# Half-array matmul pairs for kv, nd and the last rows of the two token matmuls, in a kernel of linear attention and an MLP mixer

## The chip, the cores and the metric

The kernel runs on one core of a Trainium2 chip. The metric is device time in microseconds (us), the median of several executions. All runs reported here are set against runs of the kernel before from the same rounds on the same chip. The profile's span is some 2 us shorter than the device time; spans are compared with spans only. The engines have these names in the profile: PE is TensorE (the 128 x 128 array that does the matmuls), ACT is ScalarE, DVE is VectorE, POOL is GpSimd, and SP issues transfers. PSUM is the memory that matmuls write to and ACT and DVE read from; a tile there is called a buffer below. A *mode* of the array is the way it is cut: whole, in two halves of 64 columns, or in two halves of 64 rows.

## The reference, cut to what matters

```python
# q, k, v: (8, 8, 576, 64)
q_p, k_p = phi(q), phi(k)                        # where(x > 0, x, exp(x) - 1) + 1
kv  = einsum('bhsd,bhse->bhde', k_p, v)          # "kv"
z   = sum(k_p, axis=2)
num = einsum('bhsd,bhde->bhse', q_p, kv)         # "nd": num and den in one matmul
den = einsum('bhsd,bhd->bhs', q_p, z)[..., None] + 1e-06
x   = (num / den) as (8, 576, 512)
h   = relu(x^T @ w_tok1) @ w_tok2                # "mm1", "mm2": over the 576 tokens
u   = x + h^T
out = u + relu(u @ w_ch1) @ w_ch2                # "mm3", "mm4": the wide ones
```

A batch has 576 = 4 x 128 + 64 tokens. The last 64 ("tail", row group R = 4) fill half of the 128 partitions; two batches share a tile for them in mm3 and mm4, so the natural period of the kernel is a **pair of batches**.

## The kernel before

Steady work is a list of wide pieces (mm3 and mm4, matmuls of 512 columns). Small pieces for the next batch are put between them by number: after wide step i come the pieces with number i, sorted in a stable way. This one order is the order of issue for every engine.

```python
def kv(n, g, first=False):                   # g: half of the heads; ps: 128 x 4*65 of PSUM
    for i in range(2):
        j = 2 * g + i                        # a pair of heads in one full matmul
        for r in range(R1):
            nc.tensor.matmul(out=ps[:, i], lhsT=kp[:, r, 2*j:2*j+2, :],
                             rhs=(vst[b] if r == R else vs[:, r])[:, 2*j:2*j+2, :],
                             start=(r == 0), stop=(r == R))
    for i in range(2):                       # only the diagonal blocks are wanted
        nc.scalar.copy(out=kvbd[b][half[i], 2*g:2*g+2, i*D1:(i+1)*D1],
                       in_=ps[half[i], :, i*D1:(i+1)*D1])

def nd_mm(n, g, rs):                         # six pieces a batch: 2 halves x ([0,1], [2,3], [4])
    for i, r in enumerate(rs):
        for a in range(2):
            nc.tensor.matmul(out=ps[:, i, ...], lhsT=qT[b][:, 2*g+a, r, :],
                             rhs=kvbd[b][:, 2*g+a, :], start=True, stop=True)
# ... nd_end (DVE): den + eps, reciprocal, multiply into x
# ... mm1: 2 x 5 matmuls of 512 columns, then two relus on ACT; mm2: DVE adds x, giving u
# ... mm2 of the tail: 2 matmuls a batch with zero-padded weights w2t, one DVE add into ut
# ... utr: 16 transposes of u, copied to uT by ACT and DVE

def run(bigs, fill):
    for i, big in enumerate(bigs):
        big()
        for s, fn in fill:
            if s == i: fn()

def fill_of(n, at, ks, qs):
    fill += [(at[nm], fn) for nm, fn in steps(n + 1)]                     # next batch
    fill += [(s, lambda g=g: prep_k(n + 2, g)) for g, s in enumerate(ks)] # ks = [10, 12]
    fill += [(s, lambda g=g: prep_q(n + 2, g)) for g, s in enumerate(qs)]
    return sorted(fill, key=lambda e: e[0])
# prep_k: ACT exp, DVE add/min/max, ACT casts of v

AT = {"kv0": 0, "kv1": 1, "qt0": 2, "qt1": 3, "nd00": 4, "nd01": 5, "nd10": 6, "nd11": 7,
      "nd20": 8, "nd21": 9, "mm1": 11, "mm2a": 14, "mm2b": 15, "mm2t": 16, "ut": 17, "utt": 19}
```

## Time and profile before

| | before |
|---|---|
| device time, median of 3 | 293.16 us (292.76 to 293.96); 293.38 with a fourth run below |
| span of the profile | 290.8 us |
| TensorE busy | 274.4 us (94%) |
| DVE, ACT busy | 58%, 57% |
| period of a pair of batches | 64.31 us |

The period is the distance between the first kv matmul of one batch and that of the batch two later, read from TensorE's timeline (132.37 and 196.68 us).

### The profile page before, as it was taken

Reading aid. Unit: us, or ns where it says so; the run is one execution under the profiler, and the core shown is the slowest. Engines: PE = TensorE matmul, PEld = TensorE weight load, DVE = VectorE, ACT = ScalarE, POOL = GpSimd, SP = SyncE. Lnnn points to the kernel's source line nnn. Section 1 sums busy time; section 2 is a strip of 40 time slices with the busy share of each in tenths; the row PEclk is TensorE's granted clock in tenths of the full one; section 3 lists DMA queues with packets and bytes.
Section 4 is the critical chain, followed back from the end, with each engine's and each line's share of the span. In section 5 each row is a group of like instructions: output and inputs, shape, how many; then the busy total and the mean of one; then the engine's idle time right before and its main releaser. Section 6 shows DMA issues by size and latency. Waiting matters only on the chain.

```text
span 290.8 us, 5019 instructions
## 1 busy us (share of the span) xinstructions
PE 274.4 (94%) x2002; PEld 156.5 (54%) x2002; DVE 168.2 (58%) x329; ACT 164.7 (57%) x254; POOL 29.3 (10%) x52
## 2 busy tenths in 40 slices
PE   8888987978999899999999999999999999999993
PEld 8776444543754465456565465456565464544641
DVE  5885377585657948692859517791769334530021
ACT  3663875139983676756696086658694185026400
POOL 3080030012000210010000210010001200000000
PEclk9999999999999999999999999999999999999999
DMA  6999999999996970785066710011001210011031
GB/s 204 280 139 202 300 241 211 293 283 359 278 291 207 287 206 2 212 239 184 0 169 204 261 39 0 36 69 42 2 0 38 108 36 2 36 72 38 1 108 72
DMA packets 46231, 41.84 MB, mean 144 GB/s; under 512 B 14656, under 2 KB 43200, under 8 KB 46208
## 3 DMA queue, kind: packets, MB, share of 16 engines
q1 hardware_dynamic: 39712, 30.68, 37.0%
q0 software_dynamic: 6496, 10.85, 15.8%
q8 instruction: 15, 0.25, 0.4%
q14 instruction: 8, 0.07, 0.1%
HBM read 35.85 MB, written 9.44 MB: 156 GB/s over the span
## 4 chain that ended last, share of the span: by engine, by line
PE 72%; DMA 11%; SPq 5%; ACT 4%; DVE 3%; issue 2%; POOL 1%; ACTq 0%
PE h_ps L359 28%; PE c_ps L336 22%; DMA q_raw<-in_q_dram 7%; PE a_ps L231 5%; PE h_ps L242 4%; DMA wc<-in_moe_w_ch_dram 3%; SPq L106 3%; PE nd_ps L196 3%; PE c_ps L347 3%; SPq L104 2%; PE tp L173 2%; PE tp L259 2%; PE kv_ps L163 2%; ACT e L116 2%; DMA k_raw<-in_k_dram 1%
## 5 line engine op out<-in xcount | busy, mean ns | idle before, releaser
L336 PE MATMUL c_ps<-uT,wc 128*128 128x512 bf16 x384 | 92.8, 379 | 2.4 <-ACT cr L340 1.5
L359 PE MATMUL h_ps<-wc,cr 128*128 128x512 bf16 x384 | 90.4, 379 | 0.0
L340 ACT ACTIVATE cr<-c_ps 128x512 bf16<-128x512 f32 x96 | 56.5, 599 | 47.4 <-PE c_ps L336 47.1
L359 PEld LDWEIGHTS <-cr 128*128 128x128 bf16 x384 | 36.5, 98 | 39.5
L336 PEld LDWEIGHTS <-wc 128*128 128x128 bf16 x384 | 35.4, 97 | 35.6 <-issue 3.3
L369 DVE TENSOR_TENSOR o_sb<-h_ps,u 128x512 f32<-128x512 f32 x32 | 21.8, 685 | 20.2 <-PE h_ps L359 20.1
L373 POOL DMA_DIRECT2D out_dram<-o_sb x24 | 14.4, 601 | 164.1 <-DVE o_sb L369 142.3
L209 DVE TENSOR_TENSOR x<-nd_ps,den 128x512 bf16<-128x512 f32 (+1 forms) x48 | 28.9, 603 | 1.7
L130 DVE TENSOR_SCALAR e<-e 128x1280 bf16<-128x1280 bf16 (+1 forms) x34 | 16.1, 474 | 22.0 <-ACT e L116 22.0
L206 DVE TENSOR_SCALAR den<-nd_ps 128x8 f32<-128x8 f32 (+1 forms) x48 | 7.8, 162 | 34.9 <-PE nd_ps L196 34.4
L116 ACT ACTIVATE e<-k_raw 128x1280 bf16<-128x1280 f32 x16 | 20.3, 1270 | 3.3 <-DMA k_raw<-in_k_dram 3.2
L116 ACT ACTIVATE e<-q_raw 128x1280 bf16<-128x1280 f32 (+1 forms) x18 | 20.3, 1150 | 2.8 <-DMA q_raw<-in_q_dram 2.7
L263 ACT COPY uT<-tp 128x1024 bf16<-128x1024 bf16 x7 | 7.1, 1012 | 25.0 <-PE tp L259 25.0
L248 DVE TENSOR_TENSOR u<-h_ps,x 128x1024 bf16<-128x1024 f32 x14 | 16.5, 1218 | 4.8 <-PE h_ps L242 4.8
L196 PEld LDWEIGHTS <-qT 128*128 128x128 bf16 x160 | 12.5, 98 | 11.8 <-ACT qT L187 1.2
L187 ACT COPY qT<-tp 128x1280 bf16<-128x1280 bf16 x14 | 17.2, 1231 | 1.6 <-PE tp L173 1.6
L196 PE MATMUL nd_ps<-kvbd,qT 128*128 128x130 bf16 x160 | 16.8, 221 | 0.9 <-ACT kvbd L167 0.5
L234 ACT ACTIVATE ar<-a_ps 128x512 bf16<-128x512 f32 x14 | 7.5, 592 | 15.7 <-PE a_ps L231 15.7
L122 DVE TENSOR_SCALAR y<-k_raw 128x1280 bf16<-128x1280 f32 x16 | 13.2, 823 | 3.9 <-DMA k_raw<-in_k_dram 3.7
L144 ACT CAST vs<-v_raw 128x1024 bf16<-128x1024 f32 x14 | 14.8, 1055 | 0.0
L394 PE MATMUL bank<-identity 128*128 128x128 bf16 x168 | 13.3, 247 | 1.4 <-POOL identity masks.py:199 1.4
L242 PE MATMUL h_ps<-ar,w 128*128 128x512 bf16 x56 | 14.4, 379 | 0.1
(88 smaller groups left out, 287.3 us busy)
## 6 DMA issues: line engine op xcount, KB each, us to landing
k_raw<-in_k_dram SPq DMA_DIRECT2D x16, 512.0 KB, 5.3
q_raw<-in_q_dram SPq DMA_DIRECT2D x16, 512.0 KB, 6.6
v_raw<-in_v_dram SPq DMA_DIRECT2D x16, 512.0 KB, 6.9
out_dram<-o_sb POOLq DMA_DIRECT2D x24, 256.0 KB, 2.9
wc<-in_moe_w_ch_dram POOLq DMA_DIRECT2D x8, 384.0 KB, 8.2
out_dram<-o_sb SPq DMA_DIRECT2D x8, 256.0 KB, 2.4
k_raw<-in_k_dram SPq DMA_DIRECT2D x16, 64.0 KB, 5.2
q_raw<-in_q_dram SPq DMA_DIRECT2D x16, 64.0 KB, 6.2
```

What stands on the lines that cost most here:

```text
L116: nc.scalar.activation(out=e, in_=f, func=AF.Exp)
L130: nc.vector.tensor_scalar(out=e, in0=e, scalar1=1.0, scalar2=None, op0=ALU.min)
L144: copy(out=vs[:, :, hs, 0:D].transpose([0, 2, 1, 3]), in_=raw["v", b][:, hs, 0:R])
L187: nc.scalar.copy(out=qT[b][:, 2 * g:2 * g + 2].rearrange("p j r c -> p (j r) c"), in_=tp[:, 0:2 * R1])
L196: nc.tensor.matmul(out=ps[:, i, a * 2 * D1:(a + 1) * 2 * D1], lhsT=qT[b][:, j, r, :], rhs=kvbd[b][:, j, :], start=True, stop=True)
L209: nc.vector.tensor_tensor(out=x[b][:, rs[0]:rs[0] + m, HG * D * g:HG * D * (g + 1)].rearrange("p r (h d) -> p r h d", h=HG), in0=v_[:, :, ...
L242: nc.tensor.matmul(out=ps[:, i], lhsT=w2t[:, kt, b, :] if r == R else w2v[:, kt, r], rhs=ar[b][:, kt, :], start=(kt == 0), stop=(kt == NT ...
L248: nc.vector.tensor_tensor(out=u[b][:, rs[0]:rs[0] + m], in0=ps[:, 0:m], in1=x[b][:, rs[0]:rs[0] + m], op=ALU.add)
L336: nc.tensor.matmul(out=ps, lhsT=wc1[:, kj, 128 * mc:128 * mc + 128], rhs=uT[b][:, kj].rearrange("p r c -> p (r c)"), start=(kj == 0), stop ...
L340: nc.scalar.activation(out=cr[b][:, mc, :], in_=ps, func=AF.Relu)
L359: nc.tensor.matmul(out=ps, lhsT=crt[:, kc, :] if t == 8 else cr[b][:, kc, 128 * r:128 * r + 128], rhs=wc2[:, kc, :], start=(kc == 0), stop ...
L369: nc.vector.tensor_tensor(out=o, in0=ps, in1=ut[p % 2] if t == 8 else u[b][:, r, :], op=ALU.add)
```

## The change

The full array computes more than is wanted: kv takes two off-diagonal blocks along, nd multiplies by zeros, and the tail matmuls multiply zero-padded weights. The change runs each of these as pairs of matmuls on the two halves of the array: kv and the tail of mm2 on 64-column halves, nd and the tail of mm1 on 64-row halves. The tail of mm2 is done once for both batches of a pair. nd becomes one piece for each row group r, over all heads.

```diff
 def kv(n, g, first=False):
+    for i in range(2):
+        for r in range(R1):
+            for a in range(2):
+                h = 2 * (2 * g + i) + a
+                nc.tensor.matmul(out=ps[half[a], i], lhsT=kp[:, r, h, :],
+                                 rhs=(vst[b] if r == R else vs[:, r])[:, h, :], ...)
+    nc.scalar.copy(out=kvd[b][:, 2 * g:2 * g + 2], in_=ps)
+def nd_mm(n, rs, j0, nj):
+    for i, r in enumerate(rs):
+        for j in range(nj):
+            for a in range(2):
+                nc.tensor.matmul(out=ps[:, a, at:at + D1], lhsT=qT[b][half[a], j0 + j, r, :],
+                                 rhs=kvd[b][half[a], j0 + j, :], start=True, stop=True)
 # mm1: 2 x 4 full matmuls, then
+    for mt in range(NT):
+        nc.tensor.matmul(out=ps[:, mt], lhsT=w1t[half[mt]], rhs=x[b][half[mt], R, :], ...)
+def mm2_tail(p):                             # once a pair of batches
+    for kt in range(NT):
+        for b in range(2):
+            nc.tensor.matmul(out=ps[half[b]], lhsT=w2[:, kt, SM:S], rhs=ar[b][:, kt, :], ...)
+    for b in range(2):
+        nc.vector.tensor_tensor(out=ut[p % 2][half[b]], in0=ps[half[b]], in1=x[b][half[b], R], ...)
 # load: the tail of q goes to both halves of the partitions (16 transfers more)
-    AT = {..., "nd00": 4, "nd01": 5, "nd10": 6, "nd11": 7, "nd20": 8, "nd21": 9, "mm1": 11, ...
+    AT = {..., "nd0": 4, "nd1": 5, "nd2": 6, "nd3": 7, "nd4": 8, "mm1": 10, ...
```

Cuts: the first batch's own code, its warm-up (92 full matmuls in place of 82 full ones and 20 halves), the memsets and w2t copies that go, nd_end (DVE's work on one row group over all heads), and the renumbering in the loops of the first two batches.

More of the change, by code (lines that the diff above doesn't have):

```diff
@@ L63 @@
     w1 = const("w1", [128, R, DTOK])
-    w1t = const("w1t", [128, 2, DTOK])
+    w1t = const("w1t", [128, 128])
     w2 = const("w2", [128, NT, S])
-    w2t = const("w2t", [128, NT, 2, 128])
     wc1 = const("wc1", [128, NDM, DCH])
@@ L76 @@
     qT = [const(f"qT{b}", [128, HP, R1, 128]) for b in range(2)]
-    kvbd = [const(f"kvbd{b}", [128, HP, 2 * D1]) for b in range(2)]
+    kvd = [const(f"kvd{b}", [128, HP, D1]) for b in range(2)]
     x = [const(f"x{b}", [128, R1, DM]) for b in range(2)]
@@ L105, in load @@
                                       in_=s.rearrange("p h r d -> p h (r d)")), gate)
-        nc.sync.dma_start(out=dst[half[b], hs, R, :],
-                          in_=src[nm][n, hs, SM:S, :].transpose([1, 0, 2]))
+        for i in range(2):
+            if nm == "q" or i == b:
+                nc.sync.dma_start(out=dst[half[i], hs, R, :],
+                                  in_=src[nm][n, hs, SM:S, :].transpose([1, 0, 2]))
         return ins
@@ L155, in kv @@
         if first:
-            ps = bank()[:, 0:4 * D1].rearrange("p (j e) -> p j e", j=2)
+            ps = bank()
         else:
-            ps = ps_sm.tile([128, 2, 512], FP32, name="kv_ps", tag="sm")[:, 0, 0:4 * D1].rearrange(
-                "p (j e) -> p j e", j=2)
+            ps = ps_sm.tile([128, 2, 512], FP32, name="kv_ps", tag="sm")[:, 0]
+        ps = ps[:, 0:2 * D1].rearrange("p (j e) -> p j e", j=2)
         for i in range(2):
-            j = 2 * g + i
             for r in range(R1):
-                nc.tensor.matmul(out=ps[:, i], lhsT=kp[:, r, 2 * j:2 * j + 2, :],
-                                 rhs=(vst[b] if r == R else vs[:, r])[:, 2 * j:2 * j + 2, :],
-                                 start=(r == 0), stop=(r == R))
-        for i in range(2):
-            nc.scalar.copy(out=kvbd[b][half[i], 2 * g:2 * g + 2, i * D1:(i + 1) * D1],
-                           in_=ps[half[i], :, i * D1:(i + 1) * D1])
+                for a in range(2):
+                    h = 2 * (2 * g + i) + a
+                    nc.tensor.matmul(out=ps[half[a], i], lhsT=kp[:, r, h, :],
+                                     rhs=(vst[b] if r == R else vs[:, r])[:, h, :],
+                                     start=(r == 0), stop=(r == R))
+        nc.scalar.copy(out=kvd[b][:, 2 * g:2 * g + 2], in_=ps)
     def qtr_pair(n, j, tp, put):
@@ L188, in qtr @@
                        in_=tp[:, 0:2 * R1])
-    def nd_mm(n, g, rs):
+    def nd_mm(n, rs, j0, nj):
         b = n % 2
@@ L193, in nd_mm @@
         for i, r in enumerate(rs):
-            for a in range(2):
-                j = 2 * g + a
-                nc.tensor.matmul(out=ps[:, i, a * 2 * D1:(a + 1) * 2 * D1],
-                                 lhsT=qT[b][:, j, r, :], rhs=kvbd[b][:, j, :],
-                                 start=True, stop=True)
-        live["nd", g, rs[0]] = ps
-    def nd_end(n, g, rs):
+            for j in range(nj):
+                at = D1 * (nj * i + j)
+                for a in range(2):
+                    nc.tensor.matmul(out=ps[:, a, at:at + D1], lhsT=qT[b][half[a], j0 + j, r, :],
+                                     rhs=kvd[b][half[a], j0 + j, :], start=True, stop=True)
@@ L202, in nd_end @@
+        live["nd", j0, rs[0]] = ps
+    def nd_end(n, rs, j0, nj):
         b = n % 2
-        m = len(rs)
-        v_ = live["nd", g, rs[0]][:, 0:m, 0:HG * D1].rearrange("p r (h e) -> p r h e", h=HG)
-        den = work.tile([128, 2, HG], FP32, name="den", tag="den")[:, 0:m]
-        nc.vector.tensor_scalar(out=den, in0=v_[:, :, :, D:D1].rearrange("p r h o -> p r (h o)"),
+        m = nj * len(rs)
+        v_ = live["nd", j0, rs[0]][:, :, 0:m * D1].rearrange("p a (i e) -> p a i e", i=m)
+        den = work.tile([128, 2, 4], FP32, name="den", tag="den")[:, :, 0:m]
+        nc.vector.tensor_scalar(out=den, in0=v_[:, :, :, D:D1].rearrange("p a i o -> p a (i o)"),
@@ L207, in nd_end @@
                                 scalar1=EPS, scalar2=None, op0=ALU.add)
         nc.vector.reciprocal(out=den, in_=den)
-        nc.vector.tensor_tensor(
-            out=x[b][:, rs[0]:rs[0] + m, HG * D * g:HG * D * (g + 1)].rearrange(
-                "p r (h d) -> p r h d", h=HG),
-            in0=v_[:, :, :, 0:D],
-            in1=den[:, :, :, None].to_broadcast([128, m, HG, D]), op=ALU.mult)
-    def nd(n, g, rs):
-        nd_mm(n, g, rs)
-        nd_end(n, g, rs)
-    ALL = slice(0, DM)
-    COLS = [slice(0, DM // 2), slice(DM // 2, DM)]
+        for i, r in enumerate(rs):
+            js = slice(nj * i, nj * i + nj)
+            nc.vector.tensor_tensor(
+                out=x[b][:, r, 2 * D * j0:2 * D * (j0 + nj)].rearrange(
+                    "p (j a d) -> p a j d", j=nj, a=2),
+                in0=v_[:, :, js, 0:D],
+                in1=den[:, :, js, None].to_broadcast([128, 2, nj, D]), op=ALU.mult)
@@ L223, with nd @@
+    def nd(n, r):
+        nd_mm(n, [r], 0, HP)
+        nd_end(n, [r], 0, HP)
     w2v = w2[:, :, 0:SM].rearrange("k t (p r) -> k t r p", r=R)
@@ L228, in mm1 @@
         for mt in range(NT):
-            ms = slice(128 * mt, 128 * mt + 128)
-            for r in range(R1):
-                nc.tensor.matmul(out=ps[:, mt], lhsT=w1t[:, b, ms] if r == R else w1[:, r, ms],
-                                 rhs=x[b][:, r, :], start=(r == 0), stop=(r == R))
+            for r in range(R):
+                nc.tensor.matmul(out=ps[:, mt], lhsT=w1[:, r, 128 * mt:128 * mt + 128],
+                                 rhs=x[b][:, r, :], start=(r == 0), stop=False)
+        for mt in range(NT):
+            nc.tensor.matmul(out=ps[:, mt], lhsT=w1t[half[mt]], rhs=x[b][half[mt], R, :],
+                             start=False, stop=True)
         for mt in range(NT):
@@ L241, in mm2 @@
             for kt in range(NT):
-                nc.tensor.matmul(out=ps[:, i], lhsT=w2t[:, kt, b, :] if r == R else w2v[:, kt, r],
-                                 rhs=ar[b][:, kt, :], start=(kt == 0), stop=(kt == NT - 1))
-        if rs[0] == R:
+                nc.tensor.matmul(out=ps[:, i], lhsT=w2v[:, kt, r], rhs=ar[b][:, kt, :],
+                                 start=(kt == 0), stop=(kt == NT - 1))
+        nc.vector.tensor_tensor(out=u[b][:, rs[0]:rs[0] + m], in0=ps[:, 0:m],
+                                in1=x[b][:, rs[0]:rs[0] + m], op=ALU.add)
+    def mm2_tail(p):
+        ps = ps_sm.tile([128, 2, DM], FP32, name="h_ps", tag="sm")[:, 0]
+        for kt in range(NT):
+            for b in range(2):
+                nc.tensor.matmul(out=ps[half[b]], lhsT=w2[:, kt, SM:S], rhs=ar[b][:, kt, :],
+                                 start=(kt == 0), stop=(kt == NT - 1))
+        for b in range(2):
             h = half[b]
-            nc.vector.tensor_tensor(out=ut[n // 2 % 2][h], in0=ps[h, 0], in1=x[b][h, R], op=ALU.add)
-        else:
-            nc.vector.tensor_tensor(out=u[b][:, rs[0]:rs[0] + m], in0=ps[:, 0:m],
-                                    in1=x[b][:, rs[0]:rs[0] + m], op=ALU.add)
+            nc.vector.tensor_tensor(out=ut[p % 2][h], in0=ps[h], in1=x[b][h, R], op=ALU.add)
     def utr(n, js):
@@ L278, in mm1_first @@
         if rs[0] == 0:
-            live["mm1"] = bank().rearrange("p (t c) -> p t c", t=NT) if g == 0 else ps_sm.tile(
-                [128, NT, 512], FP32, name="a_ps", tag="sm")[:, :, 0:DM // 2]
-        ps = live["mm1"]
+            live["mm1"] = [bank()[:, 0:DM // 2] for _ in range(NT)]
         for mt in range(NT):
-            ms = slice(128 * mt, 128 * mt + 128)
             for r in rs:
-                nc.tensor.matmul(out=ps[:, mt], lhsT=w1t[:, 0, ms] if r == R else w1[:, r, ms],
-                                 rhs=x[0][:, r, cs], start=(r == 0), stop=(r == R))
+                if r < R:
+                    nc.tensor.matmul(out=live["mm1"][mt],
+                                     lhsT=w1[:, r, 128 * mt:128 * mt + 128],
+                                     rhs=x[0][:, r, cs], start=(r == 0), stop=False)
         if rs[-1] == R:
-            nc.scalar.activation(out=ar[0][:, :, cs], in_=ps, func=AF.Relu)
+            for mt in range(NT):
+                nc.tensor.matmul(out=live["mm1"][mt], lhsT=w1t[half[mt]],
+                                 rhs=x[0][half[mt], R, cs], start=False, stop=True)
+            for mt in range(NT):
+                nc.scalar.activation(out=ar[0][:, mt, cs], in_=live["mm1"][mt], func=AF.Relu)
     def mm2_first(g, rs, add):
@@ L394, in warm @@
             nc.tensor.matmul(out=ps[:, 0:128], lhsT=identity, rhs=identity, start=True, stop=True)
-    def warm_half(m):
-        ps = bank()
-        for i in range(m):
-            h = half[i % 2]
-            nc.tensor.matmul(out=ps[h, 0:D1], lhsT=identity[:, h], rhs=identity[:, 0:D1],
-                             start=True, stop=True)
     landed = {}
@@ L407 @@
     nc.scalar.activation(out=one, in_=one, func=AF.Exp)
-    for nm in "kq":
-        nc.vector.memset(raw[nm, 0][half[1], :, R, :], 0.0)
+    nc.vector.memset(raw["k", 0][half[1], :, R, :], 0.0)
     for g in range(2):
@@ L417 @@
         nc.vector.memset(vst[b][half[b], :, D:D1], 1.0)
-        nc.vector.memset(kvbd[b], 0.0)
-    nc.gpsimd.memset(w1t, 0.0)
-    nc.gpsimd.memset(w2t, 0.0)
-    for nm in "kq":
-        nc.gpsimd.memset(raw[nm, 1][half[0], :, R, :], 0.0)
+    nc.gpsimd.memset(raw["k", 1][half[0], :, R, :], 0.0)
     NB = 4
@@ L438 @@
     phi("k", 0, 0, HG)
-    warm(60)
-    warm_half(20)
-    warm(22)
+    warm(92)
     phi_exp("q", 0, 0, 2)
@@ L452 @@
     warm(6)
-    nd_mm(0, 0, [0, 1])
-    nd_mm(0, 0, [2, 3])
+    nd_mm(0, [0, 1], 0, 2)
+    nd_mm(0, [2, 3], 0, 2)
     phi_exp("k", 0, HG, HG)
     phi_add("k", 0, HG, HG)
-    nd_end(0, 0, [0, 1])
+    nd_end(0, [0, 1], 0, 2)
     warm(30)
-    nd_mm(0, 0, [4])
+    nd_mm(0, [4], 0, 2)
     warm(30)
@@ L464 @@
         out=w1, in_=moe_w_tok1[0:SM, :].rearrange("(p r) t -> p r t", r=R)), landed["q", 1])
-    nc.gpsimd.dma_start(out=w1t[half[0], 0, :], in_=moe_w_tok1[SM:S, :])
+    for mt in range(NT):
+        nc.gpsimd.dma_start(out=w1t[half[mt]], in_=moe_w_tok1[SM:S, 128 * mt:128 * mt + 128])
     nc.gpsimd.dma_start(out=w2, in_=moe_w_tok2.rearrange("(k p) s -> p k s", p=128))
     c_in = [load_wc1(i) for i in range(NB)]
-    nc.gpsimd.dma_start(out=w1t[half[1], 1, :], in_=moe_w_tok1[SM:S, :])
     c2_in = [load_wc2(0)]
@@ L479 @@
     kv(0, 1, True)
-    nd_end(0, 0, [2, 3])
-    nd_end(0, 0, [4])
+    nd_end(0, [2, 3], 0, 2)
+    nd_end(0, [4], 0, 2)
     warm(8)
-    nd_mm(0, 1, [0, 1])
-    nd_end(0, 1, [0, 1])
-    nd_mm(0, 1, [2, 3])
-    nd_end(0, 1, [2, 3])
+    nd_mm(0, [0, 1], 2, 2)
+    nd_end(0, [0, 1], 2, 2)
+    nd_mm(0, [2, 3], 2, 2)
+    nd_end(0, [2, 3], 2, 2)
     mm1_first(0, range(R1))
-    nd_mm(0, 1, [4])
-    nd_end(0, 1, [4])
+    nd_mm(0, [4], 2, 2)
+    nd_end(0, [4], 2, 2)
     mm2_first(0, [0, 1], True)
@@ L510 @@
             load(nm, 2, g, c2_in[2] if nm == "k" and g == 0 else None)
-    def w2_tails():
-        for kt in range(NT):
-            for b in range(2):
-                nc.scalar.copy(out=w2t[:, kt, b, half[b]], in_=w2[:, kt, SM:S])
     def steps(n):
@@ L521, in steps @@
         out_ += [(f"qt{g}", lambda g=g: qtr(n, g)) for g in range(2)]
-        for i, rs in enumerate(([0, 1], [2, 3], [4])):
-            for g in range(2):
-                out_.append((f"nd{i}{g}", lambda g=g, rs=rs: nd(n, g, rs)))
+        out_ += [(f"nd{r}", lambda r=r: nd(n, r)) for r in range(R1)]
         out_ += [("mm1", lambda: mm1(n)), ("mm2a", lambda: mm2(n, [0, 1])),
-                 ("mm2b", lambda: mm2(n, [2, 3])), ("mm2t", lambda: mm2(n, [R])),
-                 ("ut", lambda: utr(n, [0, 1]))]
+                 ("mm2b", lambda: mm2(n, [2, 3]))]
+        if n % 2:
+            out_.append(("mm2t", lambda: mm2_tail(n // 2)))
+        out_.append(("ut", lambda: utr(n, [0, 1])))
         if n % 2:
@@ L562 @@
         [lambda kc=kc: m4_0(kc) for kc in range(NCH)]
-    at0 = {"kv0": 11, "kv1": 11, "qt0": 14, "qt1": 15, "nd00": 16, "nd01": 17, "nd10": 18,
-           "nd11": 19, "nd20": 20, "nd21": 21, "mm1": 22, "mm2a": 23, "mm2b": 23, "mm2t": 23,
+    at0 = {"kv0": 11, "kv1": 11, "qt0": 14, "qt1": 15, "nd0": 16, "nd1": 17, "nd2": 18,
+           "nd3": 19, "nd4": 20, "mm1": 22, "mm2a": 23, "mm2b": 23, "mm2t": 23,
            "ut": 23, "utt": 23}
-    fill = [(0, w2_tails), (2, lambda: mm2(0, [R]))]
-    fill += [(5, lambda: phi("k", 1, 0, HG)), (7, lambda: phi("k", 1, HG, HG)),
+    fill = [(5, lambda: phi("k", 1, 0, HG)), (7, lambda: phi("k", 1, HG, HG)),
              (9, lambda: vcast(1, 0, nc.vector.tensor_copy)),
@@ L582 @@
     big = m3(1) + m3t + m4(0, [4, 5, 6, 7, 8])
-    at1 = {"kv0": 10, "kv1": 11, "qt0": 13, "qt1": 14, "nd00": 15, "nd01": 16, "nd10": 17,
-           "nd11": 18, "nd20": 19, "nd21": 20, "mm1": 22, "mm2a": 24, "mm2b": 25, "mm2t": 26,
+    at1 = {"kv0": 10, "kv1": 11, "qt0": 13, "qt1": 14, "nd0": 15, "nd1": 16, "nd2": 17,
+           "nd3": 18, "nd4": 19, "mm1": 21, "mm2a": 24, "mm2b": 25, "mm2t": 26,
            "ut": 27}
@@ L591 @@
     run(big, sorted(fill, key=lambda e: e[0]))
-    AT = {"kv0": 0, "kv1": 1, "qt0": 2, "qt1": 3, "nd00": 4, "nd01": 5, "nd10": 6, "nd11": 7,
-          "nd20": 8, "nd21": 9, "mm1": 11, "mm2a": 14, "mm2b": 15, "mm2t": 16, "ut": 17, "utt": 19}
+    AT = {"kv0": 0, "kv1": 1, "qt0": 2, "qt1": 3, "nd0": 4, "nd1": 5, "nd2": 6, "nd3": 7,
+          "nd4": 8, "mm1": 10, "mm2a": 14, "mm2b": 15, "mm2t": 16, "ut": 17, "utt": 19}
     for n in range(2, B):
```

## The prediction

> **What bounds the kernel now.** I read the table of windows first (columns: stretch and its length in us; busy time and instructions of TensorE, weight loads, DVE, ACT, POOL; granted clock; DMA share; GB/s):
>
> ```profile
> 0.00:24.00 24.00, 20.09 (x276) 18.52 (x277) 18.51 (x47) 12.79 (x20) 9.50 (x19) 1.00 0.93 207
> 24.00:64.00 40.00, 34.86 (x230) 18.56 (x229) 23.22 (x45) 19.27 (x33) 2.83 (x4) 1.00 1.12 258
> 64.00:100.00 36.00, 33.21 (x240) 18.15 (x239) 24.98 (x47) 26.55 (x40) 4.46 (x7) 1.00 0.97 287
> 100.00:166.40 66.40, 66.40 (x464) 36.68 (x462) 44.65 (x84) 42.85 (x64) 6.03 (x11) 1.00 0.56 166
> 166.40:230.70 64.30, 64.30 (x449) 35.58 (x448) 40.52 (x77) 41.29 (x62) 5.46 (x10) 1.00 0.11 38
> ```
>
> There are two regimes. Up to about 64 us the DMA is saturated (share near 1) and TensorE has holes; from 100 us on TensorE has no idle time, while DVE and ACT are near 65% and DMA is slack. A busy row can hide slow issue, so I went to TensorE's timeline next (start, length in us, then what). One stretch of batch work (kv, and one nd group):
>
> ```profile
> 167.10 0.39 PE L163 MATMUL kv_ps<-vs,kp 128*128 128x130 bf16 x4
> ...
> 167.67 1.03 PE L336 MATMUL c_ps<-uT,wc 128*128 128x512 bf16 x4
> ...
> 172.81 0.40 PE L196 MATMUL nd_ps<-kvbd,qT 128*128 128x130 bf16 x4
> 173.04 1.02 PE L336 MATMUL c_ps<-uT,wc 128*128 128x512 bf16 x4
> 173.90 0.39 PE L196 MATMUL nd_ps<-kvbd,qT 128*128 128x130 bf16 x4
> ```
>
> Distances of starts are the price, not the lengths (0.22 us or more, which overlap). Ten kv matmuls take 167.67 - 167.10 = 0.57 us, 0.057 each. Four nd matmuls take 173.04 - 172.81 = 0.23 us, again 0.057. Four 512-column matmuls take 173.90 - 173.04 = 0.86, 0.216 each. The stream is gapless, at the pace of its columns: any array time taken away or added here shows at the end one for one. The chain of waits says the same: from 101 us it runs on TensorE nearly unbroken.
>
> **What the Trainium skill says.** "TensorEngine Tiling (Array Packing)", section Key Properties: tiles of the array run in parallel, and changing the tiling mode, as opposed to the tile, drains the engine. Its section Restrictions adds that column tiling switches Fast Weight Load off. "TensorE: Matmul & The Clock Gate", Part 3, says that matmuls on different tiles run concurrently, some 4 ns apart in start. The kernel before has one place that tests all three: its warm-up has 20 matmuls on alternating 64-column halves (L400) between full ones (L394):
>
> ```profile
> 6.89 0.50 PE L394 MATMUL bank<-identity 128*128 128x128 bf16 x6
> 7.32 0.51 PE L400 MATMUL bank<-identity 128*64 128x65 bf16 x20
> 7.75 0.34 PE L394 MATMUL bank<-identity 128*128 128x128 bf16 x3
> ```
>
> It agrees with the first two points. One half matmul lasts 0.195 us, so the last of the 20 starts at 7.32 + 0.51 - 0.195 = 7.635, and 19 steps take 0.315 us: 0.0166 each, 0.033 a pair, against 0.057 for one full 130-column matmul. So halves do run side by side. But the last full matmul before started at 6.89 + 0.50 - 0.22 = 7.17, so entering cost 0.15 instead of 0.056, and leaving cost 7.75 - 7.635 = 0.115 instead of about 0.03. Each change of mode costs about 0.1 us in which nothing streams. All in all, from 7.17 to the last start of the third row (7.87) there are 0.70 us, of which three full matmuls are 0.168: the 20 halves took **0.53 to 0.54 us** with both changes, of which 10 x 0.033 stream and **0.21** is the two changes. On weight loads: 64-column ones last 0.111 us against 0.098 of full ones, but keep up with 0.033 a pair, so they don't limit.
>
> **The change part by part.** The array program is known: 336 matmuls become 64-column halves and 338 become 64-row halves. The trace of before has no 64-row pair; that it paces and drains like a column pair is my assumption, an estimate. Per batch in the gapless part:
>
> - kv: two groups, each 10 full matmuls (0.567) become 10 pairs in one block (0.33 + 0.21 = 0.54). Saves 2 x 0.027 = 0.05.
> - nd: before, 20 matmuls of 130 columns in six groups with no mode change: 20 x 0.057 = 1.13. After, five groups, each 4 pairs standing alone between full 512-column matmuls: 5 x (4 x 0.033 + 0.21) = 1.71. Costs 0.58. The streaming falls by 0.47, but five drains in and out cost 1.05.
> - mm1's last rows: two 512-column matmuls (0.432) become one pair (0.216 + 0.21 = 0.43). Nothing.
> - mm2's last rows: once a pair of batches, two column pairs (0.43 + 0.21 = 0.64) in place of four full ones (0.86). Saves 0.22 a pair, 0.11 a batch.
>
> Sum: -0.05 + 0.58 + 0 - 0.11 = **+0.42 us a batch**, 0.84 a pair of 64.3 us. Batches 3 to 7 lie wholly in the gapless part; batch 2 lies in 64 to 100 us, where TensorE is idle for 2.8 us and part of it disappears. I count 5.5 batches: +2.3 us. Batch 1's nd steps (48 to 54 us) also run back to back with wide matmuls; with its kv groups adjacent, so sharing one block, I put +0.3.
>
> Off the array: the q tail is now loaded to both halves, one more transfer on the SP queue for each q load. In the start the chain runs through this queue:
>
> ```profile
> 5.30 1.26 SPq L106
> 6.61 6.95 DMA q_raw<-in_q_dram
> ...
> 34.92 7.31 DMA q_raw<-in_q_dram
> ```
>
> Issues stand back to back at 0.6 to 0.65 us each. Ahead of the second q transfer of batch 0 there is one more issue, so +0.65 us; the landing of that q releases the weight loads, which release batch 1's loads. Ahead of batch 1's second q transfer there is one more again, +0.65. That is up to +1.3 us, if nothing else is later; the extra 64 KB pieces also share a saturated DMA.
>
> In the other direction: ACT loses one of the two 0.27 us kv evacuations per group, and the w2t copies (0.67 us at 29.7 us); the memsets that go (4 on POOL and DVE) stand before data lands. mm1 of batch 0 gets two relus in place of one, each half as wide. DVE trades six den groups (4 x 1.1 + 2 x 0.8 us) for five of about 1.1, hidden under TensorE. I take -0.3 us for all this, a choice.
>
> Total: 293.2 + 2.3 + 0.3 + 1.3 - 0.3 = **296.8 us**.
>
> **The rivals.**
>
> (a) The drain is hidden or absent for 64-row pairs, above all between 512-column matmuls. Then nd costs 5 x 0.132 = 0.66 instead of 1.71, mm1 saves 0.2, and a batch is 0.85 us shorter than before: 293.2 - 4.7 + 1.3, about 290. With no drain anywhere the streaming saved is 0.47 + 0.47 + 0.22 + 0.22 = 1.37 a batch, some 8 us: 286. For it speaks only that a row mode was never measured here. Against it: both changes at L400 show the full 0.1[...].
>
> (b) The 64-row pairs don't overlap, or their 128-column weights can't follow at 0.033 a pair, and a pair costs 0.057 or more. Then nd is another 0.5 us a batch dearer, total about 299.5 to 300: slower by over 2%. Against it: different rows feed different partitions and two banks, and full weight loads keep up with at least 0.057.
>
> (c) ACT or DVE becomes the bound, or the two small PSUM buffers do. An nd step now lasts 0.86 + 0.34 = 1.2 us against about 1.1 of DVE work, so it gets looser; I give this little.
>
> (d) The start is DMA-bound by bytes, not by issue, and the extra q pieces cost more (2 us) or vanish in other waits (0). This moves the total by 1.3 up or down.
>
> **Range and chances.** The drain figure comes from one place of the trace, two changes; an error of 0.05 us in a block's 0.21, times 8.5 blocks a batch and 5.5 batches, is 2.3 us. Together with (d), and with (a) for the row pairs at perhaps one in five, that gives 292.5 to 300.3 us for 8 in 10. Faster by 2% (under 287.3) needs rival (a) in full, rows and columns: 6%. Slower by 2% (over 299.0) needs (b), or dearer drains with a worse start: 22%. Within 2%: 72%.
>
> **What would show it.** In TensorE's timeline after the change: an nd group of 8 half matmuls between wide ones should shift the next wide start by 0.33 to 0.36 us; if 0.15, (a) holds; if 0.45, (b). A kv group should take 0.54 against 0.57. The period of a pair of batches should grow from 64.3 to about 65.1 us, TensorE still without a waiting engine before it, and the first weight load of each block should start about 0.1 us after the last columns of the full matmul before it have gone in. The start (to the first c_ps of batch 1 at 63.6 us) should be 1 to 2 us later, with the q_raw transfers of batch 0 and 1 landing 0.6 and 1.3 us later. A pair shorter than 64.3 us would make the prediction wrong in its core; a start that isn't later would make only its smaller half wrong.

## More of the kernel before

The prediction shows the windows and the timeline lines of this kernel. One view it doesn't show is ACT's timeline around mm1 of one batch (start, length in us; in brackets the idle time before and what ended it).

```profile
179.34 0.60 ACT L340 ACTIVATE cr<-c_ps 128x512 bf16<-128x512 f32 x1 [0.38 <-PE c_ps L336]
179.83 1.26 ACT L116 ACTIVATE e<-k_raw 128x1280 bf16<-128x1280 f32 x1
180.99 1.05 ACT L144 CAST vs<-v_raw 128x1024 bf16<-128x1024 f32 x1
181.93 0.40 ACT L145 CAST vst<-v_raw 64x256 bf16<-64x256 f32 x1
182.23 0.59 ACT L340 ACTIVATE cr<-c_ps 128x512 bf16<-128x512 f32 x1
182.72 1.06 ACT L234 ACTIVATE ar<-a_ps 128x512 bf16<-128x512 f32 x2
```

The reader is to see the order: the exp of the next k (L116), the casts of v, the relu of the last mm3 (L340), and only then the two relus of mm1 (L234). While mm1 runs on TensorE, ACT has other work to do.

## The result, and the profile after

The changed kernel takes **306.75 us** (306.38 to 307.05, 4 runs) against 293.38 us of the kernel before (4 runs): ratio 1.0456, 95% interval 1.0429 to 1.0482. It is slower by 4.6%, well outside the predicted 292.5 to 300.3. Here and below a ratio is the mean time of one kernel's runs over that of the other's of the same rounds, so not quite the ratio of the medians quoted.

The table of windows of the changed kernel (columns as in the prediction), cut at the first kv matmuls of every second batch:

```profile
64.00:103.70 39.70, 36.88 (x301) 19.10 (x305) 28.73 (x50) 28.20 (x40) 5.02 (x8) 1.00 1.07 295
103.70:173.80 70.10, 65.24 (x519) 32.65 (x528) 41.96 (x75) 40.16 (x58) 5.46 (x10) 1.00 0.53 156
173.80:243.90 70.10, 65.43 (x521) 32.63 (x530) 39.96 (x71) 40.16 (x58) 5.46 (x10) 1.00 0.10 36
```

A pair of batches takes 70.1 us instead of 64.3, and TensorE, which had no idle time here, now has 4.7 us of it. The span grew by 14.0 us (290.8 to 304.8). The marks of the timeline say where: until batch 3's kv 0.9 us (102.79 to 103.73), in the two pairs that follow 11.5 us (128.62 to 140.15), after that 1.5 us. So most of it is a matter of the steady part, not of the start.

The array did what was counted. One stretch of nd in TensorE's timeline:

```profile
180.35 1.04 PE L346 MATMUL c_ps<-uT,wc 128*128 128x512 bf16 x4
181.32 0.30 PE L197 MATMUL nd_ps<-kvd,qT 64*128 64x65 bf16 x8
181.56 1.04 PE L346 MATMUL c_ps<-uT,wc 128*128 128x512 bf16 x4
182.53 0.30 PE L197 MATMUL nd_ps<-kvd,qT 64*128 64x65 bf16 x8
```

From one nd group to the next it is 182.53 - 181.32 = 1.21 us, of which four wide matmuls are 0.86: a group costs about 0.35 us by these rounded starts (0.34 by the trace's nanoseconds), predicted 0.34. The last wide matmul before it started at 180.35 + 1.04 - 0.38 = 181.01, and the first half at 181.32: 0.31 instead of 0.216, so the change of mode into row pairs costs 0.095 us, just like that into column pairs (where the traces have the same distance, 0.309 us).

What was not counted stands in the list of TensorE's waits for one pair of batches (us in total, times, longest; it counts waits over 0.15 us, and a sixth line, 0.2 us of "issue", is cut). The same list for the kernel before, over a pair, is empty:

```profile
PE tp L266 <- DVE u L245: 1.5, 2, 0.8
PE nd_ps L197 <- ACT qT L187: 1.0, 2, 0.5
PE h_ps L369 <- ACT cr L350: 0.7, 1, 0.7
PE h_ps L252 <- DVE u L245: 0.4, 1, 0.4
PE tp L266 <- DVE ut L256: 0.4, 1, 0.4
```

These are five kinds of wait for ACT and DVE, seven waits in all, though both are less busy over the span than before (DVE 165.1 us against 168.2, ACT 159.7 against 164.7). ACT's timeline around mm1 shows why:

```profile
187.10 0.60 ACT L350 ACTIVATE cr<-c_ps 128x512 bf16<-128x512 f32 x1 [0.27 <-PE c_ps L346]
189.16 1.09 ACT L235 ACTIVATE ar<-a_ps 128x512 bf16<-128x512 f32 x2 [1.46 <-PE a_ps L232]
190.13 1.27 ACT L117 ACTIVATE e<-k_raw 128x1280 bf16<-128x1280 f32 x1
191.29 1.05 ACT L145 CAST vs<-v_raw 128x1024 bf16<-128x1024 f32 x1
192.23 0.41 ACT L146 CAST vst<-v_raw 64x256 bf16<-64x256 f32 x1
192.53 0.59 ACT L350 ACTIVATE cr<-c_ps 128x512 bf16<-128x512 f32 x1
```

The relus of mm1 (L235) now stand ahead of the exp (L117). They can't start before mm1 ends on TensorE, so ACT idles for 1.46 us while the exp, ready to go, queues behind. The exp starts at 190.13 instead of right after the relu at 187.10. DVE, in order too, waits for it:

```profile
191.43 0.49 DVE L131 TENSOR_SCALAR e<-e 128x1280 bf16<-128x1280 bf16 x1 [4.29 <-ACT e L117]
...
196.19 2.34 DVE L245 TENSOR_TENSOR u<-h_ps,x 128x1024 bf16<-128x1024 f32 x2
```

The last mm3 relu (L350 at 192.53) is late for mm4, and DVE's adds into u are late for the next pieces. The place of mm1 was moved from number 11 to 10 as nd had one piece fewer, and number 10 is that of prep_k, behind which it now sorts first.

### The profile page after: what moved, and what is told of

The parts are those of the page before. It is cut to its first block, busy times and chain, and to the rows that moved or that the text cites. A ratio compares the mean times of both kernels' runs of the same rounds, so it can differ in the third digit from the quotient of the medians.

```text
span 304.8 us, 5592 instructions
## 1 busy us (share of the span) xinstructions
PE 278.0 (91%) x2274; PEld 146.9 (48%) x2312; DVE 165.1 (54%) x309; ACT 159.7 (52%) x236; POOL 26.9 (9%) x49
## 4 chain that ended last, share of the span: by engine, by line
PE 57%; DMA 12%; ACT 11%; DVE 8%; SPq 5%; issue 4%; POOL 1%; ACTq 0%
PE h_ps L369 24%; PE c_ps L346 19%; DMA q_raw<-in_q_dram 8%; ACT qT L187 5%; PE a_ps L229 4%; DVE u L245 4%; SPq L107 3%; PE nd_ps L197 3%; DMA wc<-in_moe_w_ch_dram 3%; PE c_ps L357 3%; ACT cr L350 3%; SPq L103 2%; ACT e L117 2%; DVE ut L256 2%; PE tp L266 2%
## 5 line engine op out<-in xcount | busy, mean ns | idle before, releaser
L350 ACT ACTIVATE cr<-c_ps 128x512 bf16<-128x512 f32 x96 | 56.5, 599 | 56.3 <-PE c_ps L346 55.6
L346 PEld LDWEIGHTS <-wc 128*128 128x128 bf16 x384 | 33.8, 98 | 39.0 <-issue 5.1
L211 DVE TENSOR_TENSOR x<-nd_ps,den 128x512 bf16<-128x512 f32 (+1 forms) x45 | 28.1, 631 | 1.4
L206 DVE TENSOR_SCALAR den<-nd_ps 128x8 f32<-128x8 f32 (+1 forms) x41 | 6.7, 164 | 39.6 <-PE nd_ps L197 37.8
L117 ACT ACTIVATE e<-q_raw 128x1280 bf16<-128x1280 f32 (+1 forms) x18 | 20.3, 1150 | 4.5 <-DMA q_raw<-in_q_dram 3.3
L117 ACT ACTIVATE e<-k_raw 128x1280 bf16<-128x1280 f32 x16 | 20.4, 1273 | 4.0 <-DMA k_raw<-in_k_dram 3.8
L235 ACT ACTIVATE ar<-a_ps 128x512 bf16<-128x512 f32 x14 | 7.6, 594 | 22.8 <-PE a_ps L232 22.8
L197 PEld LDWEIGHTS <-qT 64*128 64x128 bf16 x320 | 7.6, 95 | 19.5 <-DVE den L208 8.9
L197 PE MATMUL nd_ps<-kvd,qT 64*128 64x65 bf16 x320 | 13.2, 194 | 3.5 <-ACT qT L187 3.2
L404 PE MATMUL bank<-identity 128*128 128x128 bf16 x178 | 14.0, 247 | 1.4 <-POOL identity masks.py:199 1.4
L123 DVE TENSOR_SCALAR y<-q_raw 128x1280 bf16<-128x1280 f32 x16 | 13.3, 829 | 2.3 <-DMA q_raw<-in_q_dram 2.1
```

The costliest lines, as they stand in the source:

```text
L117: nc.scalar.activation(out=e, in_=f, func=AF.Exp)
L123: nc.vector.tensor_scalar(out=y, in0=f, scalar1=1.0, scalar2=None, op0=ALU.add)
L197: nc.tensor.matmul(out=ps[:, a, at:at + D1], lhsT=qT[b][half[a], j0 + j, r, :], rhs=kvd[b][half[a], j0 + j, :], start=True, stop=True)
L211: nc.vector.tensor_tensor(out=x[b][:, r, 2 * D * j0:2 * D * (j0 + nj)].rearrange("p (j a d) -> p a j d", j=nj, a=2), in0=v_[:, :, js, 0:D] ...
L346: nc.tensor.matmul(out=ps, lhsT=wc1[:, kj, 128 * mc:128 * mc + 128], rhs=uT[b][:, kj].rearrange("p r c -> p (r c)"), start=(kj == 0), stop ...
L350: nc.scalar.activation(out=cr[b][:, mc, :], in_=ps, func=AF.Relu)
```

## The experiments

**Theory**: mm1's relus in front of prep_k in the order of ACT and DVE cost most of it; nd0, which now needs the qT of all heads, costs the next part. **Rival 1**: the mode changes of the array cost more than counted. **Rival 2**: the extra q transfers. The period of a pair is the distance between the first kv matmuls of batches 4 and 6, counted from 0, in each profile.

| run | median us | before us | ratio (95%) | period of a pair |
|---|---|---|---|---|
| before | 293.38 | | | 64.31 |
| changed | 306.75 | 293.38 | 1.0456 (1.0429 to 1.0482) | 70.08 |
| mm1_slot11 | 301.18 | 293.25 | 1.0269 (1.0218 to 1.0319) | 66.93 |
| prep_first | 301.06 | 293.25 | 1.0268 (1.0218 to 1.0319) | 66.93 |
| nd_late | 304.34 | 293.25 | 1.0382 (1.0336 to 1.0428) | 68.78 |
| both | 297.64 | 293.25 | 1.0161 (1.0114 to 1.0208) | 65.63 |
| both_ut18 | 297.57 | 292.83 | 1.0153 (1.0111 to 1.0195) | 64.95 |
| before_mm1_10 | 299.39 | 292.96 | 1.0222 (1.0190 to 1.0254) | 67.67 |
| before_kv_pairs | 293.48 | 292.96 | 1.0006 (0.9978 to 1.0034) | 64.23 |
| before_nd_pairs | 297.18 | 292.96 | 1.0146 (1.0113 to 1.0179) | 65.41 |
| nd_grouped | 296.68 | 292.83 | 1.0119 (1.0085 to 1.0153) | 65.05 |
| before_q_tail2 | 294.02 | 292.89 | 1.0041 (1.0022 to 1.0060) | 64.32 |
| before_kv_mm2t | 293.67 | 292.96 | 1.0017 (0.9985 to 1.0049) | 64.09 |
| kv_mm2t_ut18 | 291.16 | 292.83 | 0.9937 (0.9907 to 0.9966) | 63.41 |

All gave correct results.

### mm1_slot11: mm1 back at its number

```diff
-    AT = {... "nd4": 8, "mm1": 10, ...
+    AT = {... "nd4": 8, "mm1": 11, ...
```

> The changed kernel with one number undone: in the steady loops mm1 of the next batch is again issued after wide step 11, not 10. Theory (the relu of mm1 stands in ACT's order ahead of the exp of the next k, waits for mm1's end, and everything behind it on ACT and DVE comes late): the waits of TensorE for cr (0.88 us) and for u and ut (1.85 us in one batch, about 0.5 + 0.55 in the other) go, 3.8 us a pair of batches in two pairs, about 7.6 us: 299 us. Rival (the mode changes of the array cost more than counted, or the rows of mm1 as pairs do it): nothing changes, 306 to 307 us.

Measured 301.18 us, and a period of 66.93 instead of 70.08. Rival 1 would have left the time as it was: every pair and every mode change is still there. The gain was 5.6 us where 7.6 was expected: 3.15 us a pair instead of 3.8, because 0.37 and 0.29 us a pair of the waits for ut and u remain, which are not of this cause (see both_ut18).

### prep_first: the same order on TensorE, another on ACT and DVE

```diff
-            fill += [(s, lambda g=g: prep_k(n + 2, g)) for g, s in enumerate(ks)]
+            fill = [(s, lambda g=g: prep_k(n + 2, g)) for g, s in enumerate(ks)] + fill
```

> The changed kernel; TensorE's order is as it was, with mm1 after step 10. Only where two pieces share a step, the preparation of k and v (exp, casts) is issued before mm1 and its relu, so ACT and DVE do it first. If ACT's and DVE's order is the cause: as far down as with mm1 at step 11, 299 us (298 to 301). If mm1's place among TensorE's work is the cause: 306 to 307 us.

Measured 301.06 us and a period of 66.93, the same as mm1_slot11 to a hundredth. mm1 still follows wide step 10 on TensorE here; only the two pieces at number 10 changed places. ACT's timeline:

```profile
185.60 0.60 ACT L350 ACTIVATE cr<-c_ps 128x512 bf16<-128x512 f32 x1 [0.27 <-PE c_ps L346]
186.10 1.26 ACT L117 ACTIVATE e<-k_raw 128x1280 bf16<-128x1280 f32 x1
187.26 1.04 ACT L145 CAST vs<-v_raw 128x1024 bf16<-128x1024 f32 x1
188.19 0.41 ACT L146 CAST vst<-v_raw 64x256 bf16<-64x256 f32 x1
188.50 1.07 ACT L235 ACTIVATE ar<-a_ps 128x512 bf16<-128x512 f32 x2
```

The exp follows the relu at once, and the 1.46 us of idling are gone. So it is the order on ACT and DVE that costs, not where mm1 stands among the matmuls.

### before_mm1_10: the same move in the kernel before

```diff
-          "nd20": 8, "nd21": 9, "mm1": 11, "mm2a": 14
+          "nd20": 8, "nd21": 9, "mm1": 10, "mm2a": 14
```

> The kernel before, one number changed: mm1 of the next batch issued after step 10 instead of 11; no change to the array's work. Theory (ACT's order): the same cascade of waits without a single pair of halves, plus 5 to 8 us: 298 to 301 us. Rival (the pairs and their drains are the cause): 293 to 294 us.

Measured 299.39 us and a period of 67.67. Without one pair of halves, the kernel before loses 3.36 us a pair to this one number. Its ACT timeline has the same hole in front of the same relu:

```profile
182.56 0.60 ACT L340 ACTIVATE cr<-c_ps 128x512 bf16<-128x512 f32 x1 [0.38 <-PE c_ps L336]
184.71 1.09 ACT L234 ACTIVATE ar<-a_ps 128x512 bf16<-128x512 f32 x2 [1.56 <-PE a_ps L231]
185.69 1.27 ACT L116 ACTIVATE e<-k_raw 128x1280 bf16<-128x1280 f32 x1
```

The hole is 1.56 us against 1.46 in the changed kernel, so it doesn't come from mm1's tail being done as a pair at the end.

### nd_late: nd one step later

```diff
-    AT = {... "nd0": 4, "nd1": 5, "nd2": 6, "nd3": 7, "nd4": 8, "mm1": 10, ...
+    AT = {... "nd0": 5, "nd1": 6, "nd2": 7, "nd3": 8, "nd4": 9, "mm1": 10, ...
```

> The changed kernel with the five nd steps one step later (5 to 9 instead of 4 to 8), mm1 still at 10. Theory: nd0 needs the qT of both halves of the heads, which ACT copies one step too late; each batch loses 0.56 us to it. Six batches: minus 3.3 us, if mm1 doesn't then wait for the last nd (it follows after one wide step, 0.86 us, and DVE needs about 1.1): 303.5 us, up to 305. Rival (nd's cost is drains): no change, 306.7.

Measured 304.34 us and 68.78 us a pair: minus 1.30 a pair, 0.65 a batch. In the changed kernel nd0 stands one wide step after the second transpose, and its matmuls of the second half of the heads wait for ACT's copy of qT (1.23 us long). This line is from the changed kernel:

```profile
180.19 0.23 PE L197 MATMUL nd_ps<-kvd,qT 64*128 64x65 bf16 x4 [0.48 <-ACT qT L187]
```

Before, the first nd piece took the first half of the heads only, whose qT had been ready for a step.

### both, and both_ut18: the two mended, and a third

```diff
-    AT = {... "nd0": 4 ... "nd4": 8, "mm1": 10, "mm2a": 14, "mm2b": 15, "mm2t": 16, "ut": 17, "utt": 19}
+    AT = {... "nd0": 5 ... "nd4": 9, "mm1": 11, "mm2a": 14, "mm2b": 15, "mm2t": 16, "ut": 17, "utt": 19}   # both
+    AT = {... "nd0": 5 ... "nd4": 9, "mm1": 11, "mm2a": 14, "mm2b": 15, "mm2t": 16, "ut": 18, "utt": 20}   # both_ut18
```

> The changed kernel with nd at steps 5 to 9 and mm1 at 11. Theory: both waits go, 306.75 - 7.6 - 3.3 = 295.9 us; what is left over the kernel before is mode changes (0.4 us a batch) and the start. Rival (drains): stays above 303.

> The changed kernel with nd at 5 to 9, mm1 at 11, and the transposes of u one wide step later (18 instead of 17; the tail's at 20). In the run with the first two, TensorE still waited 0.37 and 0.29 us a pair of batches for ut and u there. Theory: these go too, the period of a pair falls from 65.63 to about 65.0 us, 1.6 us in all: 296 us; what is left is the mode changes (0.84 us a pair by the count) and the start. Rival: the transposes wait for something else: no change, 297.6.

both took 297.64 us and 65.63 us a pair. The two causes add up: 70.08 - 65.63 = 4.45, the sum of 3.15 and 1.30. In both, TensorE still waits for u and ut. By the order of issue, in a batch without an mm2 tail the transposes follow sooner on DVE's adds than before, and in the other the tail has two adds of 0.69 us one after the other in place of one. both_ut18 gives these transposes one step more, and its period is 64.95, minus 0.68 as expected. In the two pairs from batch 4 to 6 and from 5 to 7 the list of TensorE's waits is then empty: what it loses there beyond the pace of its columns is the mode changes. The median fell by next to nothing, though, to 297.57, so this third cause shows in the period only: the four runs scatter from 295.51 to 299.27, and the profiled one, the slowest of them, reached batch 3's kv only at 107.53 us, against 104.26 in the profile of both. That scatter is of the start and is left open below.

### before_kv_pairs and before_nd_pairs: one part of the change alone

```diff
 # before_kv_pairs: kv as in the change, evacuated into the old block-diagonal tile
+            nc.scalar.copy(out=kvbd[b][half[i], 2*g:2*g+2, i*D1:(i+1)*D1], in_=ps[half[i]])
 # before_nd_pairs: nd as in the change at numbers 5 to 9, kv on the full array
+            nc.scalar.copy(out=kvd[b][half[i], 2*g:2*g+2, :], in_=ps[half[i], :, i*D1:(i+1)*D1])
```

> The kernel before with kv alone as pairs of 64-column matmuls, all else kept (the two evacuations into the block diagonal too). By the count from the warm-up's halves a group takes 0.54 us instead of 0.567: minus 0.05 us a batch, minus 0.3 us in all: 292.5 to 293.5. If drains between 512-column matmuls were dearer (0.3 us a change): plus 5 us.

> The kernel before with nd alone as pairs of 64-row matmuls, one step later (5 to 9) so that nd0 doesn't wait for qT, mm1 kept at step 11. By the count (5 x 0.34 us instead of 1.13 us): plus 0.58 us a batch, six batches that count: plus 3.5 us: 296 to 297.5. If the pairs' drains were the main cost of the whole change: 300 or more.

kv alone: 64.23 us a pair, minus 0.08 where 0.10 was counted; in the time that can't be told from nothing. nd alone: 65.41, plus 1.10 where 1.16 was counted, and 297.18 us. So the price of a block, taken from 20 warm-up matmuls, holds for column pairs and for row pairs. nd as pairs is a loss because each of its five groups of only four pairs pays for two mode changes.

### nd_grouped: fewer mode changes, the same matmuls

The diff is against before_nd_pairs:

```diff
-    AT = {... "nd0": 5, "nd1": 6, "nd2": 7, "nd3": 8, "nd4": 9, "mm1": 11, ...
+    AT = {... "nd0": 5, "nd1": 5, "nd2": 7, "nd3": 7, "nd4": 9, "mm1": 11, ...
```

> The kernel before with nd as pairs of 64-row matmuls, but in three blocks a batch instead of five (two rows' groups back to back at steps 5 and 7, the last at 9): the same matmuls, four mode changes fewer a batch. If a block's two changes cost 0.21 us, the period of a pair falls from 65.41 (five blocks) to about 64.6 us, the time from 297.2 to about 295. If the changes cost nothing and the pairs themselves are slow: 65.4 and 297. Risk: two groups follow each other faster than DVE (1.1 us each) empties their two buffers; steps 7 and 9 may wait a little.

Measured 65.05 us a pair, minus 0.36, where 0.8 was expected. The four blocks that went are worth 4 x 0.21 = 0.84; of that, some 0.47 us a pair came back as waits within an nd block: twice in a pair a step from one matmul to the next takes 0.26 us where 0.03 is usual, and each time the trace has it released by DVE's multiply on the buffer (L211). That leaves 0.37, so the price of a mode change stands, and the risk named beforehand was real.

### before_q_tail2: the extra transfers alone

```diff
-        nc.sync.dma_start(out=dst[half[b], hs, R, :], in_=src[nm][n, hs, SM:S, :].transpose([1, 0, 2]))
+        for i in range(2):
+            if nm == "q" or i == b:
+                nc.sync.dma_start(out=dst[half[i], hs, R, :], in_=src[nm][n, hs, SM:S, :].transpose([1, 0, 2]))
```

> The kernel before with the change's extra transfers alone: the last 64 rows of q are loaded to both halves of the partitions (16 transfers of 64 KB more), and the two memsets that this makes needless go; the second half meets zero weights, so the result is the same. The prediction counted two more issues of 0.65 us on the chain of the start: plus 1.3 us, 294.2 us. If they hide behind the saturated transfers: within 0.5 us of before. If bytes count, not issues: plus 2 us or more.

The two memsets of q that this makes needless go too. Measured 294.02 against 292.89 us, plus 1.1 us (by the interval 0.6 to 1.8), all of it in the start: its steady period is that of the kernel before. Predicted: 1.3. Rival 2 holds with about this size and no more.

### before_kv_mm2t and kv_mm2t_ut18: what is worth keeping

```diff
 # the kernel before, with kv as pairs and mm2_tail as in the change; nd and mm1 on the full array
-    AT = {"kv0": 0, "kv1": 1, ... "mm2t": 16, "ut": 17, "utt": 19}
+    AT = {"kv0": 1, "kv1": 1, ... "mm2t": 16, "ut": 17, "utt": 19}   # before_kv_mm2t
+    AT = {"kv0": 1, "kv1": 1, ... "mm2t": 16, "ut": 18, "utt": 20}   # kv_mm2t_ut18
```

> An attempt to beat both: the kernel before with kv as pairs, both groups of heads in one step so that they share one mode (0.66 + 0.21 = 0.87 us instead of 1.13), and the last rows of mm2 once a pair of batches (saves 0.22 us a pair); nd and mm1 on the full array. By the count minus 0.26 - 0.11 = minus 0.37 us a batch, minus 2.2 us: 291 us. Risk: in the batch without the mm2 tail, the transposes of u follow sooner on DVE's adds and TensorE waits for them (0.4 us a pair), and the second kv group delays qT: then 292 to 293.5.

> Second attempt to beat both: the kernel before with kv as pairs in one block and the last rows of mm2 once a pair of batches, now with the transposes of u one wide step later. The first attempt had a period of 64.09 us a pair against 64.31, and waits of 0.66 us for u and ut there; without them 63.45 us a pair, 2.2 us in all: 291 us where the clock is full in the start, 292 where a window of it is at half. If the waits only move: 293.5.

The first attempt missed: 293.67 us, since the transposes of u waited for DVE as in both (64.09 us a pair). With these one step later the period is 63.41, expected 63.45, and the time 291.16 against 292.83 us: ratio 0.9937 (0.9907 to 0.9966). It beats both kernels, the one before by 0.6% only. The block of both kv groups in its timeline:

```profile
166.84 0.32 PE L164 MATMUL kv_ps<-vs,kp 128*64 128x65 bf16 x8
...
167.60 1.04 PE L343 MATMUL c_ps<-uT,wc 128*128 128x512 bf16 x4
```

Twenty pairs take 0.76 us from the first half to the next wide matmul, and 0.095 for the way in: 0.86 us instead of the 1.13 of 20 full matmuls. Here two mode changes serve 20 pairs; in nd, four.

## Why the prediction was wrong

Taken a pair of batches, runs show 5.13 of the 5.77 us; the last row is the remainder:

| cause | us a pair | shown by |
|---|---|---|
| mm1's relus ahead of prep_k on ACT and DVE | 3.15 | mm1_slot11, prep_first |
| nd0 waits for the second qT | 1.30 | nd_late; adds up in both |
| transposes wait for u and ut | 0.68 | both_ut18 |
| array time, with mode changes | 0.64 | what is left over the kernel before |

- **The array's part was right, if 0.2 us too high.** Counted: 0.84 us a pair. Left when every wait on the list is gone: 64.95 - 64.31 = 0.64. By parts: kv -0.08 (counted -0.10), an nd block 0.34 us (0.34), nd alone +1.10 (+1.16). Rivals (a) and (b) fall: row pairs drain as column pairs do and run side by side.
- **The start's transfers were right**: +1.1 us for the extra q pieces, counted +1.3. In the changed kernel the first c_ps of batch 1 comes at 65.05 instead of 63.61 us, in the forecast 1 to 2 us. By batch 3's kv only 0.9 us of that is left; why is not shown.
- **Two counts of the prediction are off, without weight**: 336 and 338 are the numbers of half matmuls in the changed program, not of matmuls that become halves; and six memsets go, not four.
- **The step that failed is rival (c)**: "ACT or DVE becomes the bound, or the two small PSUM buffers do. An nd step now lasts 0.86 + 0.34 = 1.2 us against about 1.1 of DVE work, so it gets looser; I give this little." It asked how much work ACT and DVE have, and they have less. It didn't ask in which order they do it. So its forecast of "TensorE still without a waiting engine before it" and of a period of 65.1 us failed: there were 4.0 us of listed waits a pair, and 70.1 us. The diff shows mm1 going from number 11 to 10, and prep_k at 10; the order of issue on ACT could have been read from the two programs before the run. An engine that does its work in order and idles for 1.46 us in front of a relu is late for everything behind it, however little it has to do. Put right, this order was worth 3.15 of the 5.77 us.
- **The sentence "any array time taken away or added here shows at the end one for one" held, but not alone.** Being gapless means that every wait put into TensorE's stream shows one for one as well, and there were seven a pair. Of these, nd0 needing the qT of all heads could have been read from the diff too: the prediction's nd item counted matmuls and drains, not what the first of them waits for.
- **Still open: the scatter of the start.** Batch 3's kv came between 102.65 and 107.53 us in the 14 profiles. both is 4.4 us over the kernel before of its rounds and both_ut18 4.7; at 2.5 pairs their steady parts make 3.3 (2.5 x 1.32) and 1.6 (2.5 x 0.64) of it, which leaves 1.1 and 3.1 us for the start and the end (the extra q pieces are 1.1 of it). So that both, at 297.6, lies close to the predicted 296.8 is in part luck. In eight of the profiles the granted clock fell to half for a window of 3.4 us or more in the first 71 us, but that does not sort them: nd_grouped, at full clock there, came at 105.08, and both and both_ut18, with two such windows each, at 104.26 and 107.53. What brings the clock down was not tested.

## What to carry to other kernels

Where an engine works in order, ask of each moved piece not only what it costs but what stands behind it in every engine's queue: one instruction that waits for the bottleneck, put ahead of work that is ready, cost five times as much here as the array's part of the change. In this kernel, halves of the array paid only in blocks long enough to carry two mode changes of 0.1 us each: a block of 20 pairs did (0.86 us against 1.13), one of four pairs did not (0.34 against 0.23). After merging pieces, look at what the first of them now waits for, and give every consumer its old distance from its producer before judging the change.

## What the Trainium skill lacked or had wrong

- "TensorEngine Tiling (Array Packing)", Key Properties, says that a change of mode drains TensorE, but no page gives its price. Here: 0.095 us on the way in, about 0.10 to 0.11 on the way out, for 64-column and 64-row pairs alike; 0.20 to 0.21 us a block, against some 0.03 us for a pair of 65-column matmuls.
- The same page, Restrictions and Gotchas: no fast weight load with column tiling. The runs fit that (0.111 us for a load of 64 columns, 0.098 for one of 128), but the page doesn't say whether it costs anything. Here it did not limit: ten pairs with their loads kept a pace of 0.033 us.
- "TensorE: Matmul & The Clock Gate", Back-to-back issue gap, gives 81 ns for N = 128 and 131 ns for N = 512 as sustained pace with a weight load for each matmul. The runs show 57 ns for 130 columns and 216 ns for 512, gapless and each with its own load: what that section calls the isolated gap is the sustained one here. The point is on that section alone: the page's Part 1 has 55.6 and 215.7 ns for matmuls back to back at N = 128 and 512, as the runs show.
- The same page, Part 1, gives a floor of about 25 ns from start to start. Between the two halves of a pair the records of five runs show 3 or 4 ns nearly always (2 to 6 at the extremes), in line with the 4 ns of the page's own Part 3.
